# Seven products of halves instead of eight for w_sp times z2, in a one-core FNet and gMLP kernel

## The chip, the cores and the metric

The kernel runs on one core of one Trainium2 chip. The metric is the device time of one execution in microseconds (us), where less is better. Five engines work side by side, each through its own instructions in order, and wait for each other by semaphores: TensorE (PE in the profile; PEld is its weight load), VectorE (DVE), ScalarE (ACT), GpSimd (POOL) and SyncE (SP), which here only issues transfers. Transfers run on 16 DMA engines. TensorE reads its operands from SBUF and sums in PSUM, which has eight banks; one bank holds a 128 x 512 float32 tile.

## What is computed

The input x is 2048 x 512 (S = 2048 rows, D = 512). Everything is float32. Cut to what matters, with `mod` standing for the six rows sa, ca, ga, sb, cb, gb made of `silu(c) @ w_mod`:

```python
h = layernorm(x) * (1 + ca) + sa
y = Cr @ (h @ Hr.T) - Ci @ (h @ Hi.T)       # DFT over 512 columns, then over 2048 rows
x = x + ga * y
h = layernorm(x) * (1 + cb) + sb
z = gelu(h @ w_in)                          # 2048 x 1792
z1, z2 = z[:, :896], layernorm(z[:, 896:])
g = w_sp @ z2 + b_sp[:, None]               # w_sp: 2048 x 2048
x = x + gb * ((z1 * g) @ w_out)             # w_out: 896 x 512
```

## The kernel before

Each float32 product is made of three matmuls on halves of the mantissa (`matmul3`): an operand is split into a high part (a ScalarE copy to float32r) and a low part (a VectorE subtraction), and high x high, high x low and low x high are summed in one PSUM bank. The low x low term is left out.

The program is one list of **steps**, numbered n. A step consumes one moving tile of 128 x 512, which is a 128-wide strip of a large matrix, transposed. `prep(n)` makes the tiles of later steps: `prep_hi(n + 3)` transposes the strip from its block on VectorE (tile `t`) and copies its high part on ScalarE (`ah`), and `prep_lo(n + 2)` subtracts for the low part on VectorE (`al`). There are 2 buffers of `t`, 4 of `ah` and 3 of `al`. A block (`stage`, 512 x 512, two buffers) holds four strips; when its last strip is transposed, `load` has SP fetch the block after the next, by four transfers of 256 KB with rows of 512 bytes. All other work hangs on step numbers: `at(n, f)` puts f behind step n's matmuls in the program, and each engine then follows the program's order.

The stages: 128 steps for the row DFT (`mm_a`, 12 matmuls each, into `gp`), with the column DFT (`mm_y`, into `yp`) between them; 16 steps for z1 (`mm_z1`), whose gelu goes to DRAM (`z1_d`, `z_d` in the profile); 16 for z2 (`mm_z2`), whose rows are normalised and split into `zh` and `zl`; and 64 steps for w_sp times z2. There `mm_w` runs over t, four quarters of 512 rows of w_sp. In a quarter, 16 steps of 7 x 3 = 21 matmuls sum all 2048 rows of z2 into seven banks (`gw`): the weights are 128 x 128 pieces of `zh` and `zl`, the moving tiles are `ah` and `al` of w_sp, and a bank holds 128 columns of z2 by 512 rows of w_sp. At a quarter's end `make_u` adds b_sp on VectorE and multiplies by z1 (on VectorE and GpSimd in turn). While the next quarter runs, `split_u` and `mm_o` multiply with w_out (84 matmuls for a quarter, into `op`), and `add_o` adds x and stores. The last quarter's output (`mm_last`) comes behind the last step.

Of the kernel before, what the change touches and what calls it, by code (L numbers as in the profile page):

```python
# [13 lines left out]
P = 128  # L14
# [5 lines left out]
def fnet_gmlp_kernel(  # L20
# [23 lines left out]

    nc = tc.nc
# [31 lines left out]

# [5 lines left out]
    def matmul3(acc, ah, al, bh, bl, first, last):  # L83
        nc.tensor.matmul(acc, ah, bh, start=first, stop=False)  # L84
        nc.tensor.matmul(acc, ah, bl, start=False, stop=False)  # L85
        nc.tensor.matmul(acc, al, bh, start=False, stop=last)  # L86
# [45 lines left out]
    src += [quad(w_sp, t, g) for t in range(NQ) for g in range(NQ)]  # L132
    NE = 4 * len(src)
# [24 lines left out]
    def prep_hi(n):  # L158
# [4 lines left out]
        if N3 <= n < N4:  # L163
# [26 lines left out]
    hpre = hp.enter_context(pool("hpre"))  # L190
# [315 lines left out]
    def mm_z2(ns):  # L506
# [12 lines left out]
        if k == ND - 1:  # L519
            z = [zrow[0].tile([P, FH], F32, tag="zrow", bufs=4, name=f"z2_{g}_{r}") for r in range(4)]  # L520
# [3 lines left out]
            for r in range(4):  # L524
# [19 lines left out]
    GW, U, UT, X2, BS, OP = {}, {}, {}, {}, {}, {}
    wo_hi, wo_lo = {}, {}

    def load_wo():
        raw = opool[0].tile([P, NF, Q], F32, tag="u", bufs=1, name="wor")
        nc.sync.dma_start(raw, w_out.rearrange("(f p) d -> p f d", p=P))
        for f in range(NF):  # L550
            wraw[f] = raw[:, f, :]
# [17 lines left out]
    def mm_w(ns):

        t, s0 = divmod(ns[0] - N4, NS)
        if s0 == 0:
            for f in range(NF):
                GW[f] = bank(f if t == 0 else (f + 7) % 8, f"gw{t}_{f}")
        a = [(s0 + k, AH.pop(n), AL.pop(n)) for k, n in enumerate(ns)]
        for f in range(NF):
            cols = slice(f * P, (f + 1) * P)
            for s, ah, al in a:
                matmul3(GW[f], z_hi[s][:, cols], z_lo[s][:, cols], ah, al, s == 0, s == NS - 1)

    def make_u(t, f):
        g = opool[0].tile([P, Q], F32, tag="g", bufs=2, name=f"g{t}_{f}")
        nc.vector.tensor_tensor(g, GW.pop(f), BS[t], op=ALU.add)  # L583
        eng = nc.vector if f % 2 else nc.gpsimd
        eng.tensor_tensor(U[t][:, f, :], U[t][:, f, :], g, op=ALU.mult)  # L585

    def make_us(t):
        for f in range(NF):
            make_u(t, f)
            if f == 3:  # L590
                prep(N4 + NS * (t + 1))

    def split_u(t, i):
        uh, ul = UT[t, i] = [opool[0].tile([P, NF, P], F32R, tag=m, bufs=1, name=f"{m}{t}_{i}") for m in ("uh", "ul")]
        nc.scalar.activation(uh, U[t][:, :, i * P:(i + 1) * P], AF.Copy)

    def split_u_lo(t, i):
        uh, ul = UT[t, i]
        nc.vector.tensor_tensor(ul, U[t][:, :, i * P:(i + 1) * P], uh.bitcast(F32), op=ALU.subtract)
# [161 lines left out]
    at(N2 + 5, p2.close)  # L761
# [113 lines left out]
```

## Time and profile before

| | before |
|---|---|
| device time, median of 3 runs | 992.02 us (991.85 to 992.44) |
| the profiled execution | 992.21 us; its span, first to last instruction, 990.4 us |
| TensorE busy | 984.5 us, 99% of the span, 4342 matmuls |
| VectorE, ScalarE, GpSimd busy | 55%, 32%, 14% |
| TensorE in the chain that ended last | 98% |
| transfers | 115.08 MB, 116 GB/s over the span |

Busy time counts when at least one instruction of an engine is in progress. Matmuls are pipelined, so one of 389 ns begins some 0.23 us after the one before it; what a matmul costs is read from the distance of starts, not from its duration. The same holds, to a smaller degree, for VectorE. In the rows of a tile's view stand the shortest, median and longest duration in ns, and the first and the last start in us.

### The profile page before, as it was taken

The numbers are of one execution on the slowest core, as the hardware profiler recorded it, in microseconds if no ns is written. First come the engines' busy times: TensorE is split into PE (matmuls) and PEld (weight loads), VectorE is DVE, ScalarE is ACT, GpSimd is POOL, SyncE is SP. The second block draws the span as 40 slices with busy tenths as digits, with TensorE's granted clock in tenths as the row PEclk, the third lists the DMA queues.
The fourth block names the chain that finished last, engine by engine and source line by source line (L and its number), as shares of the span: only waits on it lengthen the run. The fifth ranks groups of instructions, "written<-read, shape, count | busy, mean of one in ns | idle before, by whom it ended". The sixth has DMA issues, their size and how long they took to land.

```text
span 990.4 us, 11715 instructions
## 1 busy us (share of the span) xinstructions
PE 984.5 (99%) x4342; PEld 815.8 (82%) x4342; DVE 544.8 (55%) x836; ACT 312.0 (32%) x502; POOL 143.5 (14%) x282
## 2 busy tenths in 40 slices
PE   9999999999999999999999999999999999999998
PEld 6888888888888888888888998888888888888886
DVE  7799947775575446557332676566322622262315
ACT  4684424232133123223533775321111111111101
POOL 2330000214310131024311131002000200020001
PEclk9999999999999999999999999999999999999999
DMA  9996544466454535546733332444225223531131
GB/s 209 224 215 136 127 122 89 143 165 174 111 128 86 117 95 128 111 127 151 260 128 117 69 60 43 118 97 127 64 64 159 54 64 75 149 70 47 44 138 43
DMA packets 151642, 115.08 MB, mean 116 GB/s; under 512 B 11424, under 2 KB 132256, under 8 KB 151584
## 3 DMA queue, kind: packets, MB, share of 16 engines
q1 hardware_dynamic: 145088, 93.61, 41.1%
q0 software_dynamic: 6304, 20.46, 5.9%
q8 instruction: 34, 0.56, 0.2%
q10 hardware_dynamic: 192, 0.26, 0.1%
q14 instruction: 24, 0.20, 0.1%
HBM read 94.37 MB, written 19.93 MB: 115 GB/s over the span
## 4 chain that ended last, share of the span: by engine, by line
PE 98%; DMA 1%; DVE 1%; ACT 0%; POOL 0%; issue 0%; SPq 0%; DVEq 0%
PE gp L84 11%; PE gp L85 11%; PE gp L86 11%; PE gw L86 10%; PE gw L85 10%; PE gw L84 10%; PE yp L85 3%; PE yp L84 3%; PE yp L86 3%; PE z2p L84 3%; PE z2p L85 3%; PE z2p L86 3%; PE z1p L84 3%; PE z1p L86 3%; PE z1p L85 3%; PE op L86 2%
## 5 line engine op out<-in xcount | busy, mean ns | idle before, releaser
L170 ACT ACTIVATE ah<-t 128x512 fp32r<-128x512 f32 x224 | 141.5, 632 | 532.0 <-PE gw L86 211.9
L179 DVE TENSOR_TENSOR al<-t,ah 128x512 fp32r<-128x512 f32 x224 | 153.0, 683 | 270.7 <-PE gw L85 138.7
L84 PE MATMUL gp<-ah,hh 128*128 128x512 f32 x496 | 193.3, 390 | 0.0
L85 PE MATMUL gp<-al,hh 128*128 128x512 f32 x496 | 193.3, 390 | 0.0
L86 PE MATMUL gp<-ah,hl 128*128 128x512 f32 x496 | 193.2, 389 | 0.0
L86 PE MATMUL gw<-ah,zl 128*128 128x512 f32 x448 | 174.3, 389 | 0.0
L85 PE MATMUL gw<-al,zh 128*128 128x512 f32 x448 | 174.3, 389 | 0.0
L84 PE MATMUL gw<-ah,zh 128*128 128x512 f32 x448 | 174.3, 389 | 0.0
L147 DVE STREAM_TRANSPOSE t<-stage 128x512 f32<-128x512 f32 x208 | 146.4, 704 | 9.8 <-DMA stage<-in_A_dft_seq_re_dram 4.2
L84 PEld LDWEIGHTS gp<-ah,hh 128*128 128x128 f32 x496 | 93.1, 188 | 19.9
L86 PEld LDWEIGHTS gp<-ah,hl 128*128 128x128 f32 x496 | 93.1, 188 | 19.7
L85 PEld LDWEIGHTS gp<-al,hh 128*128 128x128 f32 x496 | 93.1, 188 | 19.5
L85 PEld LDWEIGHTS gw<-al,zh 128*128 128x128 f32 x448 | 84.1, 188 | 17.6
L84 PEld LDWEIGHTS gw<-ah,zh 128*128 128x128 f32 x448 | 84.1, 188 | 17.4
L86 PEld LDWEIGHTS gw<-ah,zl 128*128 128x128 f32 x448 | 84.1, 188 | 17.4
L585 POOL TENSOR_TENSOR u<-u,g 128x512 f32<-128x512 f32 x16 | 21.4, 1338 | 336.1 <-DVE g L583 336.1
L85 PE MATMUL yp<-htl,gh 128*128 128x512 f32 x128 | 51.1, 399 | 0.0
L84 PE MATMUL yp<-hth,gh 128*128 128x512 f32 x128 | 50.4, 394 | 0.0
L86 PE MATMUL yp<-hth,gl 128*128 128x512 f32 x128 | 50.1, 392 | 0.0
L85 PE MATMUL z2p<-wil,ah 128*128 128x448 f32 x128 | 46.8, 365 | 0.0
L84 PE MATMUL z2p<-wih,ah 128*128 128x448 f32 x128 | 46.7, 365 | 0.0
L86 PE MATMUL z2p<-wih,al 128*128 128x448 f32 x128 | 46.7, 365 | 0.0
(138 smaller groups left out, 1152.1 us busy)
## 6 DMA issues: line engine op xcount, KB each, us to landing
stage<-in_A_dft_seq_im_dram SPq DMA_DIRECT2D x64, 256.0 KB, 5.0
stage<-in_B_w_sp_dram SPq DMA_DIRECT2D x64, 256.0 KB, 4.7
stage<-in_A_dft_seq_re_dram SPq DMA_DIRECT2D x60, 256.0 KB, 4.8
stage<-h_d SPq DMA_DIRECT2D x32, 256.0 KB, 4.9
z_d<-z POOLq DMA_DIRECT2D x28, 256.0 KB, 5.8
u<-z_d SPq DMA_DIRECT2D x4, 1792.0 KB, 8.0
wm<-in_w_mod_dram SPq DMA_DIRECT2D x16, 256.0 KB, 5.8
xr<-in_A_x_dram POOLq DMA_DIRECT2D x16, 256.0 KB, 3.2
```

The lines of the kernel that those rows point to most:

```text
L84: nc.tensor.matmul(acc, ah, bh, start=first, stop=False)
L85: nc.tensor.matmul(acc, ah, bl, start=False, stop=False)
L86: nc.tensor.matmul(acc, al, bh, start=False, stop=last)
L147: nc.vector.transpose(dst.rearrange("p (b i) -> p b i", i=32), block[:, :, 32 * k:32 * k + 32])
L170: nc.scalar.activation(AH[n], T[n], AF.Copy)
L179: nc.vector.tensor_tensor(AL[n], T.pop(n), AH[n].bitcast(F32), op=ALU.subtract)
L585: eng.tensor_tensor(U[t][:, f, :], U[t][:, f, :], g, op=ALU.mult)
```

## The change

The four quarters become two halves, and w_sp and z2 are each cut in two both ways. Write A11, A12, A21, A22 for the 1024 x 1024 quarters of w_sp, and B11, B12, B21, B22 for those of z2, where the columns are cut into 512 and 384 (F1 and F2). Eight products of quarters would give the result; the change takes the seven of Winograd's form, with these sums (a missing 128 columns count as zero):

- of w_sp: S1 = A21 + A22, S3 = A11 - A21, S2 = S1 - A11, S4 = A12 - S2. `load_s` fetches 128 rows of both halves at a time (a unit; 16 of 1 MB), `sum_s` makes the four sums by four VectorE operations, and GpSimd's queue stores them to DRAM (`s_d`). Units 0 to 7 stand at steps 90, 94, ... 118 (in the DFT stage, in place of the pool `hpre`), units 8 to 15 at steps N2 + 6, N2 + 9, ... (the z1 and z2 stages).
- of z2: `sum_t23` and `sum_t14`, in place, by 32 VectorE operations in products 1, 7 and 4.

The products run in the order 1, 6, 7, 4, 5, 3, 2. Each takes 16 steps: eight 128-row pieces of its z2 operand times two 512-wide halves r of its w_sp operand. Products 1, 6, 4, 2 have four blocks of 128 columns (12 matmuls a step), products 7, 5, 3 three (9 a step). Banks 0 to 3 serve r = 0 and 4 to 7 serve r = 1. Products 6, 7, 4 and 3 go on summing in the banks of the product before; what stands there is first copied out by ScalarE (`keep_w`, after products 1, 6, 7, 4) or added to an earlier result by VectorE (`add_w`, after 5, 3, 2). A block of w_sp or of a sum is now 512 rows by two strips of 64 columns, loaded by eight transfers of 128 KB with rows of 256 bytes (`load_half`). The split of z2's operands into high and low is done anew for each product (`hi_b`, `lo_b`). b_sp is added on GpSimd (`add_bs`, 28 operations), w_out is scaled there (`scale_wo`), and all 16 output blocks (`mm_o`, 336 matmuls) follow the last step.

```diff
-    src += [quad(w_sp, t, g) for t in range(NQ) for g in range(NQ)]
-    NE = 4 * len(src)
+    PROD = (1, 6, 7, 4, 5, 3, 2)
+    NE = N4 + 4 * NQ * len(PROD)
+    NB = {p: N4 + 4 * NQ * i for i, p in enumerate(PROD)}
...
+            for r in range(2):
+                load_half(stage[b][:, r], s_d[S_OF[p], r, g] if p in S_OF else
+                          quad(w_sp, r + (2 if p == 4 else 0), g + (0 if p == 1 else 2)), h)
...
+    def sum_s(r, g, b, first):
+        a11, a12, a21, a22 = [SJ[r, g, b][:, i] for i in range(4)]
+        if first:
+            nc.vector.tensor_tensor(a22, a21, a22, op=ALU.add)
+            nc.vector.tensor_tensor(a21, a11, a21, op=ALU.subtract)
+            done = (1, a22), (3, a21)
+        else:
+            nc.vector.tensor_tensor(a11, a22, a11, op=ALU.subtract)
+            nc.vector.tensor_tensor(a12, a12, a11, op=ALU.subtract)
+            done = (2, a11), (4, a12)
+        for m, a in done:
+            nc.gpsimd.dma_start(s_d[m, r, g][b * P:(b + 1) * P, :], a)
...
+    def mm_w(n):
+        i, m = divmod(n - N4, 4 * NQ)
+        p, k, r = PROD[i], m // 2, m % 2
+        nf = 4 if p in (1, 6, 4, 2) else 3
+        fresh = p in (1, 5, 2)
+        if k == 0 and fresh:
+            for f in range(nf):
+                GW[r, f] = bank(4 * r + f, f"gw{p}_{r}_{f}")
+        ah, al = AH.pop(n), AL.pop(n)
+        for f in range(nf):
+            cols = slice(f * P, (f + 1) * P)
+            matmul3(GW[r, f], BH[p, k][:, cols], BL[p, k][:, cols], ah, al, fresh and k == 0, k == 7, not fresh)
+        if k == 7:
+            {1: keep_w, 6: keep_w, 7: keep_w, 4: keep_w}.get(p, add_w)(p, r)
...
+    def load_wo(f):
+        wor[f] = opool[0].tile([P, D], F32, tag="wor", bufs=2, name=f"wor{f}")
+        nc.sync.dma_start(wor[f], w_out[f * P:(f + 1) * P, :])
...
+    for i, u in enumerate((r, g, b) for g in range(2) for b in range(4) for r in range(2)):
+        n = 90 + 4 * i if i < 8 else N2 + 6 + 3 * (i - 8)
+        at(n, load_s, *u)
+        at(n + 3, sum_s, *u, True)
+        at(n + 4, sum_s, *u, False)
...
+        n = NB[3] + 2 + 2 * f
+        at(n, load_wo, f)
+        at(n + 4, scale_wo, f)
+        at(n + 6, make_wo, f)
+        at(n + 7, make_wo_lo, f)
```

How the program's order moves, at three places. First, SP's queue in the last quarter of the row DFT. Before, it holds nothing but block loads:

```order
L139 DMA stage_3002<-in_A_dft_seq_re_dram 32x16x128 x4
L139 DMA stage_3127<-in_A_dft_seq_re_dram 32x16x128 x4
L139 DMA stage_3277<-in_A_dft_seq_im_dram 32x16x128 x4
L139 DMA stage_3410<-in_A_dft_seq_im_dram 32x16x128 x4
L139 DMA stage_3508<-in_A_dft_seq_im_dram 32x16x128 x4
L139 DMA stage_3589<-in_A_dft_seq_im_dram 32x16x128 x4
```

After the change a unit of w_sp (`sj`, two transfers of 512 KB) stands ahead of each block:

```order
L572 DMA sj_3280<-in_B_w_sp_dram 128x2x512 x2
L151 DMA stage_3333<-in_A_dft_seq_im_dram 32x16x128 x4
L572 DMA sj_3439<-in_B_w_sp_dram 128x2x512 x2
L151 DMA stage_3477<-in_A_dft_seq_im_dram 32x16x128 x4
L572 DMA sj_3545<-in_B_w_sp_dram 128x2x512 x2
L151 DMA stage_3586<-in_A_dft_seq_im_dram 32x16x128 x4
```

So each DFT block is now issued behind 1 MB of w_sp, which itself waits until the stores of two units earlier have landed.

Second, VectorE during w_sp times z2. Before, in the second quarter, two or three steps' transposes (`t`) and low parts (`al`) stand between the output's operations, and each step has 21 matmuls or more:

```order
L147 STREAM_TRANSPOSE t_6330<-stage_6151 128x512
L179 TENSOR_TENSOR al_6334<-t_6295,ah_6297 128x512
L147 STREAM_TRANSPOSE t_6379<-stage_6151 128x512
L179 TENSOR_TENSOR al_6383<-t_6330,ah_6332 128x512
L607 TENSOR_TENSOR x2r_2_6328<-op_2_6357,x2r_2_6328 128x512
L147 STREAM_TRANSPOSE t_6411<-stage_6151 128x512
L179 TENSOR_TENSOR al_6415<-t_6379,ah_6381 128x512
L599 TENSOR_TENSOR ul_3_6409<-u_5920,uh_3_6408 128x896
```

After, in product 3 with its 9 matmuls a step, the low parts of z2 (`bl`) and of w_out (`wol`) stand between:

```order
L207 TENSOR_TENSOR al_7635<-t_7597,ah_7599 128x512
L677 TENSOR_TENSOR wol_7626<-wor_7494,woh_7625 128x512
L173 STREAM_TRANSPOSE t_7647<-stage_7515 128x512
L207 TENSOR_TENSOR al_7651<-t_7631,ah_7633 128x512
L613 TENSOR_TENSOR bl_6_7662<-z_3_2_5568,bh_6_7623 128x384
L173 STREAM_TRANSPOSE t_7672<-stage_7515 128x512
L207 TENSOR_TENSOR al_7676<-t_7647,ah_7649 128x512
L677 TENSOR_TENSOR wol_7667<-wor_7539,woh_7666 128x512
L173 STREAM_TRANSPOSE t_7688<-stage_7515 128x512
```

There is an operation more on every step, and a step is under half as long in matmuls.

Third, SP's queue around w_out. Before, w_out comes whole, in the first quarter:

```order
L549 DMA wor<-in_B_w_out_dram 128x7x512
L139 DMA stage_5727<-in_B_w_sp_dram 32x16x128 x4
L139 DMA stage_5860<-in_B_w_sp_dram 32x16x128 x4
L565 DMA u_5920<-z_d_84 128x7x512
L567 DMA bs_5922<-in_B_b_sp_dram 128x512
L139 DMA stage_5994<-in_B_w_sp_dram 32x16x128 x4
```

After, it comes in seven pieces (`wor`, two buffers) in products 3 and 2, between the blocks and the z1 rows (`z1t`):

```order
L666 DMA wor_7494<-in_B_w_out_dram 128x512
L157 DMA stage_7515<-s_d_01_101 32x16x64 x4
L157 DMA stage_7515<-s_d_11_103 32x16x64 x4
L666 DMA wor_7539<-in_B_w_out_dram 128x512
L658 DMA z1t_0_7575<-z_d_86 128x4x512
L666 DMA wor_7578<-in_B_w_out_dram 128x512
L658 DMA z1t_0_7595<-z_d_86 128x3x512
L157 DMA stage_7601<-in_B_w_sp_dram 32x16x64 x8
L666 DMA wor_7629<-in_B_w_out_dram 128x512
L666 DMA wor_7670<-in_B_w_out_dram 128x512
L157 DMA stage_7692<-in_B_w_sp_dram 32x16x64 x8
```

The third piece (`wor_7578`) must wait until VectorE has made `wol_7626` of the first, and the block `stage_7601` is behind it.

More of the change, by code (lines that the diff above doesn't have):

```diff
@@ L544, in fnet_gmlp_kernel, with load_s @@
[L544 to L551, printed above, removed]
+    SJ = {}
+    def load_s(r, g, b):
+        SJ[r, g, b] = spre[-1].tile([P, 4, Q], F32, tag="sj", bufs=4 if len(spre) > 1 else 2, name=f"sj{r}{g}{b}")
+        for i in range(2):
+            v = w_sp.rearrange("(i r) (j c) -> i r j c", i=2, j=2)[i]
+            o = r * Q + b * P
+            nc.sync.dma_start(SJ[r, g, b][:, 2 * i:2 * i + 2], v[o:o + P][:, :, g * Q:(g + 1) * Q])
@@ new lines, in keep_w, with add_w @@
+    def keep_w(p, r):
+        if p in (1, 4):
+            G[p, r] = spre[-1].tile([P, 4, Q], F32, tag="sj", bufs=4, name=f"g{p}_{r}")
+        else:
+            G[p, r] = gpool[0].tile([P, 3, Q], F32, name=f"g{p}_{r}")
+        for f in range(G[p, r].shape[1]):
+            nc.scalar.activation(G[p, r][:, f, :], GW[r, f], AF.Copy)
+    def add_w(p, r):
+        g = G[{5: 7, 3: 6, 2: 1}[p], r]
+        for f in range(g.shape[1]):
+            nc.vector.tensor_tensor(g[:, f, :], GW[r, f], g[:, f, :], op=ALU.add)
@@ new lines, in load_bs, with add_bs, load_z1 @@
+    def load_bs():
+        BS = gpool[0].tile([P, NQ, Q], F32, name="bs")
+        nc.sync.dma_start(BS, b_sp.rearrange("(t q) -> t q", q=Q).partition_broadcast(P))
+        for t in range(NQ):
+            wor["bs", t] = BS[:, t, :]
+    def add_bs(p, r, f):
+        g = G[p, r][:, f, :]
+        nc.gpsimd.tensor_tensor(g, g, wor["bs", r if p in (1, 6) else 2 + r], op=ALU.add)
+    def load_z1(p, r):
+        f0, f1 = (0, 4) if p in (1, 4) else (4, NF)
+        Z1T[p, r] = gpool[0].tile([P, 4, Q], F32, tag="z1t", bufs=2, name=f"z1t{p}_{r}")[:, :f1 - f0]
+        nc.sync.dma_start(Z1T[p, r], z1_d[r if p in (1, 6) else 2 + r][f0:f1].rearrange("f p t -> p f t"))
@@ L569, in mm_w @@
[L569 to L585, printed above, removed]
@@ L605, in add_o, with load_x2 @@
+    def load_x2(t):
+        last = blocks.tile([P, 4, D], F32, tag="stage", bufs=2, name=f"x2r{t}")
+        nc.sync.dma_start(last, x2_d[t].rearrange("(i p) d -> p i d", p=P))
+        for i in range(4):
+            X2[t, i] = last[:, i, :]
     def add_o(t, i):
@@ L829, in fnet_gmlp_kernel @@
-    first_part(0)
-    for f in range(NF):
-        if f + 1 < NF:
-            first_part(f + 1)
-        ul[f] = blocks.tile([P, Q], F32R, tag="al", bufs=3, name=f"ul{f}")
-        nc.vector.tensor_tensor(ul[f], U[t][:, f, :], uh[f].bitcast(F32), op=ALU.subtract)
-        for i in range(4):
-            if f == 1 and i == 3:
-                mm_last(0, 3)
-            if f or i < 3:
-                mm_last(f, i)
-        if f == 0:
-            run(NE)
-    for i in range(4):
-        X2[t, i] = last[:, i, :]
-        add_o(t, i)
+    load_x2(2)
@@ new lines, in fnet_gmlp_kernel @@
+    load_x2(3)
+    for o in range(len(order)):
+        if o == 1:
+            load_z1(1, 0)
+            load_z1(6, 0)
+        if o == 4:
+            load_z1(1, 1)
+            load_z1(6, 1)
+        if o + 1 < len(order):
+            split_u(*order[o + 1])
+            split_u_lo(*order[o + 1])
+        mm_o(*order[o], o % 2)
+        run(NE + o)
+        if o:
+            add_o(*order[o - 1])
+        if o in (4, 8):
+            load_x2(o // 4 - 1)
+        if 2 <= o < 4:
+            for f in range(2):
+                make_u(1, 0, 2 * (o - 2) + f)
+        if o == 4:
+            for f in range(3):
+                make_u(6, 0, f)
+        if 5 <= o < 7:
+            for f in range(2):
+                make_u(1, 1, 2 * (o - 5) + f)
+        if o == 7:
+            for f in range(3):
+                make_u(6, 1, f)
```

189 lines of the change are left out of this document (115 added, 74 removed).

## The prediction

> **What bounds the kernel now.** I read the page first: engines, slices, chain.
>
> ```profile
> span 990.4 us, 11715 instructions
> PE 984.5 (99%) x4342; PEld 815.8 (82%) x4342; DVE 544.8 (55%) x836; ACT 312.0 (32%) x502; POOL 143.5 (14%) x282
> ...
> PE   9999999999999999999999999999999999999998
> ...
> DVE  7799947775575446557332676566322622262315
> ...
> PEclk9999999999999999999999999999999999999999
> DMA  9996544466454535546733332444225223531131
> ...
> PE 98%; DMA 1%; DVE 1%; ACT 0%; POOL 0%; issue 0%; SPq 0%; DVEq 0%
> ```
>
> TensorE is busy in every slice at the full granted clock, and the chain that ended last is TensorE for 98%. VectorE is idle for about three quarters of the last third (slices 28 on), DMA for more. So the number of matmuls sets the time, as long as the others keep up. What one matmul costs comes from the views of the tiles `gw` and `op`, by first and last start.
>
> ```profile
> L84 PE MATMUL gw<-ah,zh x448: 389/389/393, 605.8 to 966.9; 128*128 128x512 f32 x150
> ...
> L86 PE MATMUL op<-woh,ul x112: 388/389/390, 701.5 to 986.4; 128*128 128x512 f32 x112
> ```
>
> Each tile has three such lines, so 3 x 448 + 3 x 112 = 1680 matmuls start between 605.8 and 986.4: 380.6 / 1679 = 0.2267 us each, with no gap left for waits. The duration of 389 ns is not the price; by it the whole kernel would take 1.7 ms.
>
> **The matmuls.** Seven products of 16 steps: four with 12 matmuls a step, three with 9, so 64 x 12 + 48 x 9 = 1200 `gw` matmuls for 1344. It is 144 and not the 168 of one eighth, because 7 column blocks are cut into 4 and 3. The 336 of the output stay and only move. 144 x 0.2267 = **32.6 us less**, if TensorE never waits. A step shrinks from 21 x 0.2267 = 4.76 us to 2.72 us (four blocks) or 2.04 us (three), and the rest of this part asks whether the others follow at that pace. w_sp times z2 then takes 64 x 2.72 + 48 x 2.04 = 272 us.
>
> **VectorE.** Its price per operation, from a stretch of the timeline where it runs without a pause (start, duration):
>
> ```profile
> 684.39 1.27 DVE L583 TENSOR_TENSOR g<-gw,bs 128x512 f32<-128x512 f32 x2
> ...
> 691.58 0.71 DVE L147 STREAM_TRANSPOSE t<-stage 128x512 f32<-128x512 f32 x1
> 692.21 0.65 DVE L179 TENSOR_TENSOR al<-t,ah 128x512 fp32r<-128x512 f32 x1
> 692.78 1.08 DVE L599 TENSOR_TENSOR ul<-u,uh 128x896 fp32r<-128x896 f32 x1
> 693.78 0.70 DVE L147 STREAM_TRANSPOSE t<-stage 128x512 f32<-128x512 f32 x1
> ```
>
> By starts: transpose 0.63, low part 0.57, 896 columns 1.00 (so 384 columns about 0.43, an estimate), an addition from PSUM 0.64. A step needs 1.20. GpSimd's additions disturb it:
>
> ```profile
> L585 POOL TENSOR_TENSOR u<-u,g 128x512 f32<-128x512 f32 x16 | 21.4, 1338 | 336.1 <-DVE g L583 336.1
> ...
> L179 DVE TENSOR_TENSOR al<-t,ah 128x512 fp32r<-128x512 f32 x224 | 153.0, 683 | 270.7 <-PE gw L85 138.7 <-PE gp L85 67.1 <-PE z1p L85 31.6
> ...
> L585 DVE TENSOR_TENSOR u<-u,g 128x512 f32<-128x512 f32 x12 | 14.9, 1239 | 0.4
> ```
>
> The VectorE operations of line 585 that run beside GpSimd's take 1239 ns where the like of line 179 takes 683, so a GpSimd addition costs VectorE about 0.56 us. The Trainium skill's page "SBUF — State Buffer", section "Who interferes with whom", says more: a VectorE operation with two SBUF inputs and a reading GpSimd operation exclude each other for a whole instruction. By that, an estimate is 1.3 us for each, which is rival A's upper end below.
>
> Product by product, VectorE against TensorE: a product has 16 x 1.20 = 19.2 us of steps and eight `bl` (4.6, or 3.4 with 384 columns).
> - Product 1: 23.8, 16 sums of z2 6.9, the last norms some 5.6: 36 of 43.5 us.
> - Product 6: 23.8 and 8 GpSimd additions 4.5: 28 of 43.5. Product 7: 22.6, 6 additions 3.4, three sum pairs 3.0: 29 of 32.6. Product 4: 23.8, five pairs 5.0, 3.4: 32 of 43.5.
> - Product 5: 22.6, 8 additions 4.5, 6 `add_w` 3.8: 31 of 32.6. Product 3: 22.6, 3.8, four `wol` 2.3, five `scale_wo` 2.8: 31.5 of 32.6.
> - Product 2: 23.8, 8 `add_w` 5.1, 14 `make_u` 8.0, three `wol` 1.7, the rest 2: 41 of 43.5.
>
> All fit, 5 and 3 barely; tiles made two to three steps ahead (4 to 8 us) even out bunches. I take 0 to 1 us of waits. By full durations (0.70 + 0.68 a step) products 5, 3 and 2 would lack some 2, 3 and 1.5 us: +6.5, the upper bound; below nothing there is no gain, since TensorE has no other wait to lose.
>
> **Banks handed over.** After products 1, 6, 7, 4 ScalarE copies each bank, as it does here, in 0.6 us:
>
> ```profile
> L80 ACT ACTIVATE gh<-gp x32: 578/598/611, 84.6 to 429.6; 128x512 fp32r<-128x512 f32 x32
> ```
>
> Copies of r = 0 lie beside the last step of r = 1 (2.04 us or more), and the next product needs bank 0 first. Cost 0; if ScalarE comes a whole copy late at each of five hand-overs, 3 us.
>
> **Block loads.** Rows of 256 bytes instead of 512, eight transfers a block. The trace has that size: the very first block is fetched in halves. In the window 9.3 to 11.5 us nearly all packets are of it:
>
> ```profile
> DMA packets 2002, 0.52 MB, mean 238 GB/s; under 512 B 1932, under 2 KB 1996, under 8 KB 2002
> ...
> 10.00:11.00 1.00, 1.00 (x6) 0.83 (x5) 1.00 (x3) 0.96 (x3) 0.00 (x0) 1.00 1.19 265
> 727.50:729.50 2.00, 2.00 (x10) 1.66 (x9) 0.00 (x0) 0.00 (x0) 0.00 (x0) 1.00 1.01 243
> ```
>
> The last column is GB/s: 265 with small packets, 243 in a window of a w_sp block with 512-byte rows. Bytes count, not packets, so 1.05 MB takes 4.4 us of every 8.2 us (4 x 2.04) or 10.9 us. In time from issue to landing:
>
> ```profile
> L139 SPq DMA_DIRECT2D stage<-in_B_w_sp_dram x64: 311/486/3985, 565.6 to 890.3; - x64
> ...
> DMA to landing us min/median/max: 2.3/3.7/6.2
> ```
>
> Seven issues of 0.49 us ahead and 3.7 for the last (the second row is for tiles `stage` up to 14 us, most of them the small ones): 7.1 us, where five steps lie between the issue and the first transpose of that block, 10.2 us with three column blocks. Cost 0. The page "DMA: Bandwidth & Descriptors" of the Trainium skill, section "Specifications", speaks against it: under 512 bytes a transfer doesn't reach line rate, because it reads, modifies and writes. The trace's loads into SBUF don't show it; rival C is what it would do.
>
> **SP's queue.** The wait of `wor_7578` for `wol_7626` holds block 64 (`stage_7601`) back from step 8 to about step 9.5 of product 3; its first transpose is wanted by step 13, and can slip to 15 before TensorE sees it. That leaves 3.5 steps, 7.1 us, against those 7.1 us of loading, plus the 768 KB of z1 just ahead (3.2 us at 243 GB/s). It is the tightest place: 0 to 4 us, I take 1.
>
> **Sums of w_sp.** 64 operations of 0.6 us lie beside the DFT (8 units, some 109 us) and z stages; VectorE there, third number:
>
> ```profile
> 388.00:400.00 12.00, 12.00 (x55) 9.94 (x54) 7.28 (x11) 3.49 (x6) 0.00 (x0) 1.00 0.71 152
> 400.00:412.00 12.00, 12.00 (x55) 9.93 (x54) 6.49 (x10) 2.85 (x5) 0.00 (x0) 1.00 0.55 111
> ```
>
> 12 us gain 2.9 us of VectorE (10.2 at most) and 2.3 MB of units and stores. 152 + 192 = 344 GB/s is above the 243 of block loads, though 2 KB rows run faster:
>
> ```profile
> 632.00:636.00 4.00, 4.00 (x20) 3.30 (x19) 0.69 (x1) 0.63 (x1) 0.00 (x0) 1.00 1.05 375
> ```
>
> Four steps need 1.05 / 0.243 + 2.1 / 0.375 = 9.9 of 10.9 us. At 243 for all it would be 13.0, and 2.1 us lost in each of the four units without a column DFT between: 0 to 8 us; I take 0.5, nearest to the rows of 2 KB.
>
> **The end.** 16 output blocks of 21 matmuls take 4.76 us each, against two `ul` (1.0), an `add_o` (0.7) and up to three `make_u` (1.7) on VectorE: hidden. The last addition and store stay:
>
> ```profile
> L607 DVE TENSOR_TENSOR x_last<-op,x_last x4: 691/692/692, 984.8 to 986.8; 128x512 f32<-128x512 f32 x4
> ```
>
> From 986.8 to the span's end is 3.6 us before, and as much after.
>
> **Sum.** 992.2 of the profiled execution (span 990.4 and 1.8 around it) - 32.6 + 0.5 (VectorE) + 1.0 (SP) + 0.5 (DMA) = 961.6. That execution is 0.2 above the median of 992.0, so I say **961.4 us**.
>
> **Rivals.**
> - A, VectorE becomes the bound in products 5, 3, 2 (7 too, with 1.3 us for each GpSimd addition): +6.5 to +14, 966 to 973. For it: margins of 1 to 2 us. Against: the starts above, which already stand in a dense stretch.
> - B, loads come late, behind `wor` in product 3 or behind the units in the DFT: +4 to +12, 963 to 972. For it: both sums above sit at their limit. Against: VectorE hardly waits for a load now (the transposes' whole idle time is 9.8 us):
>
> ```profile
> L147 DVE STREAM_TRANSPOSE t<-stage 128x512 f32<-128x512 f32 x208 | 146.4, 704 | 9.8 <-DMA stage<-in_A_dft_seq_re_dram 4.2 <-DMA stage<-in_A_dft_seq_im_dram 2.2 <-DVE al L179 0.8
> ```
>
> - C, the other side: small rows run far below the window at 10 us, and each of 28 blocks sets the pace. It decides at 304.7 / 28 = 10.9 us a block (now 304.7 us of `gw` matmuls), 96 GB/s. Two windows' worth of that size ran at 238 and 265, so it would need DRAM sums or the doubled count to behave otherwise. At 12 us a block: 28 x 12 - 272 = +64, 1025 us. By the skill's rule at half of 243 GB/s, an estimate, a block takes 8.6 us, and 12 x 0.5 = +6: still faster.
> - D, the change doesn't do what it says: the count of matmuls in the program is 1200, so no.
>
> **Chances.** Forecast (960 to 963.5) 0.57; A 0.16; B 0.17; C with a slower end 0.06, with a milder one (973 to 990) 0.03; within 0.2% of before, about what a measurement can tell, 0.01. Faster 0.93, same 0.01, slower 0.06. The floor, with no wait at all, is 992.0 - 32.6 = 959.4, and the runs before lie 0.6 apart; the range 958.8 to 973 leaves out C and little else.
>
> **What would show it.** Right: 1200 `gw` matmuls; TensorE busy 99%, and starts 0.2267 us apart through all seven products; VectorE dense in 5, 3 and 2 with little idle, ScalarE under half busy. A: in the waits, TensorE or its weight load waits for `al` in products 5 and 3, with VectorE at 100%. B: VectorE's transposes wait for transfers of `stage`, in product 3, product 2's start or between 290 and 400 us. C: the same in every block, and a landing of 10 us or more. The forecast fails if several waits meet, or if a wait that I put at 0 returns with each of 112 steps.

## The result: 964.4 us, 27.8 us faster

| | before | after |
|---|---|---|
| device time, median | 992.19 us (991.85 to 992.44) | 964.43 us (963.91 to 964.98, 4 runs) |
| ratio to before | | 0.972, 95% interval 0.9708 to 0.9732 |
| the profiled execution | 992.21 us | 964.28 us |
| its span | 990.4 us | 962.5 us |

The forecast was 961.4 us with a range of 958.8 to 973: the time lies in the range, 3.0 us above the forecast. It lies above the 960 to 963.5 us that had the chance of 0.57, and within the 963 to 972 of rival B. The page of the changed kernel, the same lines as shown of before:

```profile
span 962.5 us, 12362 instructions
PE 953.6 (99%) x4198; PEld 788.1 (82%) x4198; DVE 690.4 (72%) x1082; ACT 370.4 (38%) x631; POOL 218.4 (23%) x365
...
PE   8999999999999999999999999999999999999998
...
DVE  7789947785566757856555576888689699897642
...
PEclk9999999999999999999999999999999999999999
DMA  9996652666446797994778964445454456774441
...
PE 93%; DMA 2%; DVE 2%; SPq 1%; issue 1%; ACT 0%; DVEq 0%
```

There are 144 matmuls less (4198 for 4342). VectorE went from 55% to 72%: it is 60 to 90% busy and more in slices 29 to 38, where it had been 20 to 30% busy in eight of ten. TensorE's share of the chain fell from 98% to 93%, and transfers, VectorE and SP's queue took its place there. So something waits, though the tenths of the slices don't show it. Where it waits is shown by the four products behind the first three, one window each (4, 5, 3, 2; the columns are length, then busy time with the number of instructions of PE, PEld, DVE, ACT, POOL, then granted clock, DMA share, GB/s):

```profile
725.10:769.20 44.10, 43.85 (x194) 35.99 (x193) 36.66 (x53) 18.65 (x34) 11.32 (x8) 1.00 0.42 96
769.20:802.20 33.00, 32.95 (x145) 26.96 (x144) 29.28 (x41) 13.92 (x26) 8.61 (x6) 1.00 0.57 128
802.20:835.30 33.10, 33.04 (x146) 27.04 (x144) 28.79 (x46) 15.05 (x27) 5.46 (x4) 1.00 0.73 191
835.30:882.20 46.90, 44.60 (x191) 35.58 (x192) 44.26 (x70) 16.22 (x29) 4.49 (x4) 1.00 0.70 202
```

192 matmuls at 380.6 / 1679 = 0.22668 us are 43.52 us and 144 are 32.64. By the first starts of each product, to a hundredth, the time above these is: products 1, 6 and 7 together 0.07 us, product 4 0.54, product 5 0.34, product 3 0.44, product 2 3.40. That is 4.8 us in all, where the forecast had put 2.0, and nearly three quarters of it is in product 2.

There are two places. The first is the boundary of products 3 and 2. Here are SP's queue and then VectorE (start, duration, idle before in brackets):

```profile
816.09 0.38 SPq L658 DMA_DIRECT2D z1t<-z_d  x1
822.30 0.34 SPq L666 DMA_DIRECT2D wor<-in_B_w_out_dram  x1
822.70 0.42 SPq L658 DMA_DIRECT2D z1t<-z_d  x1
823.17 7.97 SPq L157 DMA_DIRECT2D stage<-in_B_w_sp_dram  x8
```

```profile
821.59 0.68 DVE L677 TENSOR_TENSOR wol<-wor,woh 128x512 fp32r<-128x512 f32 x1
...
831.55 0.71 DVE L173 STREAM_TRANSPOSE t<-stage 128x512 f32<-128x512 f32 x1 [2.57 <-DMA stage<-in_B_w_sp_dram]
...
834.70 1.87 DVE L643 TENSOR_TENSOR g<-gw,g 128x512 f32<-128x512 f32 x3
836.50 1.36 DVE L613 TENSOR_TENSOR bl<-z,bh 128x512 fp32r<-128x512 f32 x1
```

SP issues nothing from 816.5 until VectorE has made the `wol` of 821.59. Then come a piece of w_out, the z1 rows, and block 64 with its eight transfers. The block's first transpose starts at 831.55, and VectorE has waited 2.57 us for it. It doesn't win them back: from there it is busy for 32.39 of 32.45 us, and TensorE pays for what is late.

```profile
831.55:864.00 32.45, 30.09 (x128) 23.23 (x127) 32.39 (x50) 12.44 (x22) 5.49 (x4) 1.00 0.71 180
```

TensorE's own rows there, and its waits over the seven products (in total, times, longest):

```profile
835.52 0.47 PE L95 MATMUL gw<-ah,bh 128*128 128x512 f32 x1 [0.28 <-ACT bh L608]
835.83 0.39 PE L96 MATMUL gw<-al,bh 128*128 128x512 f32 x1
837.91 0.50 PE L97 MATMUL gw<-ah,bl 128*128 128x512 f32 x1 [1.69 <-DVE bl L613]
```

```profile
PE gw L97 <- DVE bl L613: 1.9, 2, 1.7
PE gw L96 <- DVE al L207: 0.3, 1, 0.3
PE gw L95 <- ACT bh L608: 0.3, 1, 0.3
```

From 835.83 to 837.91 is 2.08 us where 0.23 is usual: the low part of product 2's first piece of z2 stands behind product 3's three additions, and then takes 1.36 us instead of 0.68, while GpSimd scales two pieces of w_out (834.30 to 837.31). The sums of waits (2.5 us) are less than the 4.8, since the end of a matmul is modelled and one behind a gap has a longer duration; the starts are what counts.

The second place is at the starts of products 4 and 5, where GpSimd adds b_sp. Of product 4 first GpSimd, then VectorE beside it:

```profile
723.13 9.66 POOL L653 TENSOR_TENSOR g<-g,bs 128x512 f32<-128x512 f32 x6 [24.98 <-ACT g L637]
```

```profile
723.55 1.43 DVE L207 TENSOR_TENSOR al<-t,ah 128x512 fp32r<-128x512 f32 x1
724.90 1.65 DVE L598 TENSOR_TENSOR z<-z,z 128x384 f32<-128x384 f32 x1
726.58 1.66 DVE L599 TENSOR_TENSOR z<-z,z 128x512 f32<-128x512 f32 x1
728.16 0.70 DVE L173 STREAM_TRANSPOSE t<-stage 128x512 f32<-128x512 f32 x1
728.79 1.15 DVE L207 TENSOR_TENSOR al<-t,ah 128x512 fp32r<-128x512 f32 x1
729.87 1.77 DVE L613 TENSOR_TENSOR bl<-z,bh 128x512 fp32r<-128x512 f32 x1
```

The six additions hang on steps in the program's order, but GpSimd has nothing else that paces it: it waits 25 us for the first copy of a bank and then runs all six as one burst. Beside it VectorE's operations with two SBUF inputs take 1.2 to 1.8 us instead of 0.55 to 0.68, while its transposes keep their 0.70. TensorE then waits for that `bl`, 0.4 us more than its usual distance, at 731.7.

### The profile page after: what moved, and what is told of

The parts are those of the page before. It is cut to its first block, busy times and chain, and to the rows that moved or that the text cites. A ratio compares the mean times of both kernels' runs of the same rounds, so it can differ in the third digit from the quotient of the medians.

```text
span 962.5 us, 12362 instructions
## 1 busy us (share of the span) xinstructions
PE 953.6 (99%) x4198; PEld 788.1 (82%) x4198; DVE 690.4 (72%) x1082; ACT 370.4 (38%) x631; POOL 218.4 (23%) x365
## 4 chain that ended last, share of the span: by engine, by line
PE 93%; DMA 2%; DVE 2%; SPq 1%; issue 1%; ACT 0%; DVEq 0%
PE gp L95 12%; PE gp L96 12%; PE gp L97 12%; PE gw L97 8%; PE gw L96 8%; PE gw L95 8%; PE yp L96 3%; PE yp L95 3%; PE yp L97 3%; PE z2p L96 3%; PE z2p L95 3%; PE z2p L97 3%; PE z1p L95 3%; PE op L97 3%; PE z1p L96 3%; PE op L95 3%
## 5 line engine op out<-in xcount | busy, mean ns | idle before, releaser
L207 DVE TENSOR_TENSOR al<-t,ah 128x512 fp32r<-128x512 f32 x272 | 191.4, 704 | 134.0 <-PE gp L96 47.5
L173 DVE STREAM_TRANSPOSE t<-stage 128x512 f32<-128x512 f32 x256 | 180.1, 704 | 13.1 <-DMA stage<-in_A_dft_seq_re_dram 5.1
L97 PE MATMUL gw<-ah,bl 128*128 128x512 f32 x400 | 156.2, 391 | 2.1 <-DVE bl L613 1.9
L96 PE MATMUL gw<-al,bh 128*128 128x512 f32 x400 | 155.9, 390 | 0.3 <-DVE al L207 0.3
L95 PE MATMUL gw<-ah,bh 128*128 128x512 f32 x400 | 155.9, 390 | 0.3 <-ACT bh L608 0.3
L97 PEld LDWEIGHTS gw<-ah,bl 128*128 128x128 f32 x400 | 75.1, 188 | 19.5 <-DVE bl L613 4.0
L96 PEld LDWEIGHTS gw<-al,bh 128*128 128x128 f32 x400 | 75.1, 188 | 16.4 <-DVE al L207 1.0
L95 PEld LDWEIGHTS gw<-ah,bh 128*128 128x128 f32 x400 | 75.1, 188 | 16.3 <-ACT bh L608 0.7
L653 POOL TENSOR_TENSOR g<-g,bs 128x512 f32<-128x512 f32 x28 | 44.0, 1607 | 118.0 <-ACT g L637 118.0
L585 POOL DMA_DIRECT2D s_d<-sj x64 | 35.3, 551 | 125.6 <-DVE sj L577 91.8
```

Of the source, the lines that this page charges most:

```text
L95: nc.tensor.matmul(acc, ah, bh, start=first, stop=False, skip_group_check=go_on)
L96: nc.tensor.matmul(acc, ah, bl, start=False, stop=False, skip_group_check=go_on)
L97: nc.tensor.matmul(acc, al, bh, start=False, stop=last, skip_group_check=go_on)
L173: nc.vector.transpose(dst.rearrange("p (b i) -> p b i", i=32), block[:, :, 32 * k:32 * k + 32])
L207: nc.vector.tensor_tensor(AL[n], T.pop(n), AH[n].bitcast(F32), op=ALU.subtract)
L585: nc.gpsimd.dma_start(s_d[m, r, g][b * P:(b + 1) * P, :], a)
```

## The experiments

Two theories stood after this. **Q**: SP's queue, held by the third piece of w_out, makes block 64 late, and the rest follows. **V**: VectorE has too much to do around the boundary (additions of product 3, products with z1, low parts of w_out), and has it with the block in time as well. GpSimd's burst was a third cause, for products 4 and 5. Of the rivals on record, C (short rows) and the price of the sums of w_sp had to be settled too. "Excess" below is a product's time above its count of matmuls times 0.2267, from the profiled run.

**Three buffers for the pieces of w_out**, so that the third load waits for nothing:

```diff
-        wor[f] = opool[0].tile([P, D], F32, tag="wor", bufs=2, name=f"wor{f}")
+        wor[f] = opool[0].tile([P, D], F32, tag="wor", bufs=3, name=f"wor{f}")
```

> The changed kernel with three buffers for the pieces of w_out in place of two, so that SyncE hardly waits for VectorE's low part of an earlier piece before it can issue block 64 of w_sp. Theory Q (the queue): of the 4.7 us that TensorE lost in the seven products, product 2's 3.4 us come from block 64, which SyncE issued 4.6 us late. Then product 2 takes 43.5 to 44.3 us instead of 46.9, the transposes no longer wait 2.6 us for a transfer of w_sp, and the time is 961.0 to 961.8 us. Rival V (VectorE): at the start of product 2 VectorE has too much to do (additions from PSUM, low parts of z2 and of w_out, products with z1, held up by GpSimd's scaling of w_out), and the late block is beside the point. Then product 2 stays above 46 us and the time at 964.0 +- 0.4 us.

Measured: 963.03 us (962.15 to 963.98), ratio 0.9706 (0.9693 to 0.9719). SP's queue, TensorE's only wait from 800 us on, and VectorE behind the boundary:

```profile
818.53 8.62 SPq L157 DMA_DIRECT2D stage<-in_B_w_sp_dram  x8
```

```profile
PE gw L96 <- DVE al L207: 0.5, 1, 0.5
```

```profile
836.00:848.00 12.00, 11.34 (x47) 8.31 (x47) 12.00 (x19) 3.80 (x7) 2.59 (x2) 1.00 0.60 142
```

Block 64 is issued 4.6 us earlier, no transpose waits for w_sp, and product 3's excess is gone (0.44 to 0). But product 2 keeps 1.70 of 3.40, with VectorE busy for all of these 12 us. So Q, with block 64 in time, accounts for about half of the loss there. That the other half is VectorE's is argued from its being busy without a break; the next runs bear on it. Neither theory's forecast came out (961.0 to 961.8 us and 964.0).

**Without GpSimd's additions of b_sp and its scaling of w_out:**

```diff
-            at(NB[6] + 2 + 4 * r + f, add_bs, 1, r, f)
-            at(NB[5] + 2 + 8 * r + 2 * f, add_bs, 4, r, f)
-            if f < 3:
-                at(NB[7] + 2 + 3 * r + f, add_bs, 6, r, f)
-                at(NB[4] + 2 + 3 * r + f, add_bs, 7, r, f)
+            pass
...
-        at(n + 4, scale_wo, f)
```

> The changed kernel without GpSimd's 28 additions of b_sp and its seven products of w_out with gb: both are left out of the result. The SyncE queue is as in the changed kernel. Theory Q: the 0.5 and 0.3 us lost at the start of products 4 and 5 go, since they stand beside bursts of GpSimd additions; product 2 still loses 2.0 to 3.4 us behind block 64; time 962.0 to 963.5 us. Rival V: without GpSimd VectorE's operations with two SBUF inputs run in 0.57 to 0.68 us throughout, product 2 falls to 44 us or less, and the time to 960.0 to 961.0 us.

Measured: 961.78 us (961.46 to 962.93), ratio 0.9697 (0.9684 to 0.971). The excess of products 4, 5 and 3 is 0, that of product 2 is 2.10. SP still issues nothing until 821.34, and the transposes still wait 2.6 us for w_sp. So the 0.9 us of products 4 and 5 went with GpSimd's additions. Product 5's 0.34 isn't there each time, though: in two runs below, without the sums of w_sp and with one long wait, product 5 loses nothing while the same burst of eight additions runs. Product 2 lost 0.9 to 1.3 us less than in the changed kernel's two profiles (3.40 and, below, 3.00); `scale_wo` is the GpSimd work that lies there.

**Both at once.** Three buffers, and VectorE adds b_sp while it copies the banks, in place of ScalarE's copy and GpSimd's addition:

```diff
     def keep_w(p, r):
...
-            nc.scalar.activation(G[p, r][:, f, :], GW[r, f], AF.Copy)
+            nc.vector.tensor_tensor(G[p, r][:, f, :], GW[r, f], wor["bs", r if p in (1, 6) else 2 + r], op=ALU.add)
...
-        wor[f] = opool[0].tile([P, D], F32, tag="wor", bufs=2, name=f"wor{f}")
+        wor[f] = opool[0].tile([P, D], F32, tag="wor", bufs=3, name=f"wor{f}")
...
```

> The changed kernel with three buffers for w_out's pieces, and with b_sp added by VectorE while it takes the banks out of PSUM (in place of ScalarE's copy), so that GpSimd's 28 additions go; the result is complete. Theory Q with bursts of GpSimd as the cause of the small losses: products 4 and 5 lose under 0.1 us, product 2 under 0.8, time 960.0 to 960.8 us, 0.4% below the changed kernel. Rival V: the 28 additions more on VectorE (18 us in all) make products 5 and 2 worse by 1 to 3 us, time 963 to 966 us.

Measured: 961.93 us (960.78 to 962.63), ratio 0.9694 (0.9681 to 0.9707). That is 1.1 us more than theory Q had forecast at most, and less than rival V's 963 to 966. Its profiled run was its fastest; the excess there is 0.80 us, all in product 2, against 1.70 with three buffers alone, though nothing of the b_sp additions lay in product 2. Runs of each of these two kernels lie 1.8 us apart, so what VectorE costs in product 2 is known to about 1 us only. VectorE took 28 operations more and the kernel is faster than the changed one: an addition from PSUM keeps its duration beside GpSimd (in the changed kernel the three at 834.70 take 1.87 us while `scale_wo` runs), and no burst is left in products 4 and 5.

**Short rows in the kernel before.** Its w_sp blocks come by eight transfers of 256-byte rows, and nothing else differs.

```diff
-            load_block(stage[b], src[b])
+            if 4 * b >= N4:
+                load_block(stage[b], src[b], 0, 64)
+                load_block(stage[b], src[b], 64, P)
+            else:
+                load_block(stage[b], src[b])
```

> The kernel before, with each block of w_sp fetched by eight transfers of rows of 256 bytes instead of four of 512, and nothing else changed. If bytes count and not rows: the same time, 991.6 to 992.6 us, a block's transfers at 230 to 265 GB/s, landings of 3 to 4 us for 128 KB. If short rows ran at half rate (the rival that was forecast to make the change slower): the time stays too, since a block has 19 us here, but a landing of 128 KB takes 5 us or more, and in the window of a block the GB/s fall to 120 to 130.

Measured: 992.26 us (991.92 to 992.43) beside 992.16, ratio 1.0 (0.9991 to 1.0009). One window with a block in it, with short rows and then in the kernel before (DMA share and GB/s are the last two numbers), and how long a 128 KB transfer takes to land (median, last):

```profile
723.00:735.00 12.00, 12.00 (x55) 9.94 (x54) 4.05 (x6) 1.80 (x3) 0.00 (x0) 1.00 0.52 131
```

```profile
723.00:735.00 12.00, 12.00 (x54) 9.95 (x53) 4.25 (x6) 2.01 (x3) 0.00 (x0) 1.00 0.58 131
```

```profile
stage<-in_B_w_sp_dram SPq DMA_DIRECT2D x96, 128.0 KB, 3.1
```

Both windows hold the same bytes (131 GB/s over 12 us), and the DMA engines are no busier with short rows (0.52) than without (0.58). Between rows of 256 and of 512 bytes it is the bytes that count and not the packets, so rival C is excluded. In the changed kernel too, blocks from DRAM sums and from w_sp land alike:

```profile
stage<-s_d SPq DMA_DIRECT2D x128, 128.0 KB, 2.9
...
stage<-in_B_w_sp_dram SPq DMA_DIRECT2D x96, 128.0 KB, 3.2
```

**Without the sums of w_sp.** Neither loads, sums nor stores of units; the products read w_sp itself:

```diff
-                load_half(stage[b][:, r], s_d[S_OF[p], r, g] if p in S_OF else
-                          quad(w_sp, r + (2 if p == 4 else 0), g + (0 if p == 1 else 2)), h)
+                load_half(stage[b][:, r],
+                          quad(w_sp, r + (2 if p == 4 else 0), g + (0 if p == 1 else 2)), h)
...
-        at(n, load_s, *u)
-        at(n + 3, sum_s, *u, True)
-        at(n + 4, sum_s, *u, False)
+        pass
```

> The changed kernel without the sums of w_sp: no units are loaded, summed or stored, and products 5, 6, 7 and 3 read quarters of w_sp itself, so the result is not the reference's. If the 64 operations and 33.6 MB are hidden, as TensorE's starts in the DFT and z stages say: the same time, 964.4 +- 0.8 us. If they cost as I allowed (0.5, at most 8 us): 963.9 or as low as 956.

Measured: 963.94 us (963.73 to 964.27), ratio 0.9714 (0.9697 to 0.973), beside 964.43 and (below) 964.91 for the changed kernel. 64 VectorE operations and 34 MB of transfers (32 of 512 KB, 64 of 256 KB) cost 0.5 to 1.0 us at most, and the intervals don't tell that from nothing. The excess here is 0.56 us in product 4, nothing in product 5, and in products 3 and 2 as large as ever (0.68 and 2.94), so the loss there isn't theirs. The z1 stage's first matmul starts at 451.6 us in the changed kernel and at 451.8 before: the DFT lost nothing to the units.

**The matmuls put back.** In products 7, 5 and 3 the third column block is summed twice, 12 matmuls a step as in the others:

```diff
+        if nf == 3:
+            cols = slice(2 * P, 3 * P)
+            matmul3(GW[r, 2], BH[p, k][:, cols], BL[p, k][:, cols], ah, al, False, False, True)
```

> The changed kernel with a fourth block of matmuls again in products 7, 5 and 3 (the third block once more, which falsifies the sums): 1344 gw matmuls, as many as before, with everything else of the change in place. If the gain is the count of matmuls alone: 959.4 + 32.6 = 992.0 us plus what is lost in waits, 992.0 to 995.5; products 5 and 3 lose nothing now, since their steps have 2.72 us, and product 2 loses less than 2 us. If the change gained or lost elsewhere (the outputs gathered at the end, the sums), the time lies outside by that much.

Measured: 992.69 us (992.12 to 993.84) beside 992.3, ratio 1.0005 (0.9995 to 1.0014). The matmuls of each of the three lines stand at 448 again:

```profile
L95 PE MATMUL gw<-ah,bh x448: 388/389/395, 605.7 to 909.9; 128*128 128x512 f32 x150
```

With the count as before the time is as before, with all that the change adds. No product's excess is over 0.10 us, and TensorE's waits are gone: where a step of products 7, 5 and 3 gives the others 2.72 us instead of 2.04, they keep up. So the gain is the count alone, and the waits come from the short steps.

**Without the products with z1 for half of the result.** The 14 `make_u` of product 2 go, 8 us of VectorE by the prediction's price:

```diff
-        at(NB[2] - 2 + f, make_u, 4, 0, f)
-        at(NB[2] + 6 + f, make_u, 4, 1, f)
-        if f < 3:
-            at(NB[2] + 3 + f, make_u, 7, 0, f)
-            at(NB[2] + 11 + f, make_u, 7, 1, f)
+        pass
```

> The changed kernel without the 14 products with z1 (make_u of products 4 and 7) that VectorE does in product 2; half of the result lacks that factor. The loads of z1, the two buffers of w_out and all of SyncE's queue stay. Of product 2's 3.4 us, three buffers for w_out took away 1.7 and dropping GpSimd's operations took away 1.3, so neither theory holds alone. Theory QV (both meet: the late block leaves VectorE no lead, and VectorE's own surplus in the last two steps of product 3 and the first eight of product 2, 27.7 us of work for 25.9, keeps it from catching up): product 2 loses 1.0 to 2.0 us, the waits after 838 us go, time 962.6 to 963.6. If the surplus is not in these products but in the additions from PSUM, product 2 still loses 2.8 us or more, time 964.0 to 964.6.

Measured: 964.09 us (962.48 to 965.93), ratio 0.9715 (0.9699 to 0.9731): no gain that the runs show, and 2.91 us of excess in product 2. In the expectation's terms that is the second outcome, a surplus that isn't in the products with z1. But a cost that no theory had named is in it, as the profiled run (964.98) shows. SP issued block 64 at 823.89 (at 823.17 and, in the second profile below, 823.51 in the changed kernel), TensorE waited 1.3 us for product 3's additions and 1.0 us for `bl`, and then this (the number ahead of the last two is the granted clock):

```profile
837.02 0.40 PE L96 MATMUL gw<-al,bh 128*128 128x512 f32 x1
838.42 0.80 PE L97 MATMUL gw<-ah,bl 128*128 128x512 f32 x1 [1.00 <-DVE bl L613]
839.01 0.63 PE L95 MATMUL gw<-ah,bh 128*128 128x512 f32 x1
839.44 0.63 PE L96 MATMUL gw<-al,bh 128*128 128x512 f32 x1
```

```profile
838.00:839.00 1.00, 0.58 (x1) 0.50 (x2) 1.00 (x3) 0.00 (x0) 0.00 (x0) 0.62 1.24 278
839.00:840.00 1.00, 1.00 (x4) 0.79 (x3) 1.00 (x2) 0.64 (x1) 0.00 (x0) 0.50 0.57 119
840.00:841.00 1.00, 1.00 (x4) 0.81 (x3) 1.00 (x3) 0.00 (x0) 0.00 (x0) 0.50 0.12 22
841.00:842.00 1.00, 1.00 (x4) 0.76 (x4) 1.00 (x3) 0.00 (x0) 0.00 (x0) 0.67 0.01 2
```

For about 3.4 us (0.76 us of the first window, 0.66 of the last) the clock is halved and starts lie 0.43 us apart. Behind that TensorE never waits again. Eight distances of starts (838.42 to 841.85) take 3.43 us there instead of 1.81. By an estimate that is 1.6 of the 2.91 us, and the 1.3 that stay are what the first outcome had named (1.0 to 2.0). Of the four runs the one with a mean clock of 1.000 is also the fastest, 962.48, and the slowest, 965.93, has 0.997; but a run of the changed kernel at 0.997 took 964.59, no longer than the others. So the run doesn't decide on V; the last experiment measures the halved clock by itself.

**VectorE relieved at the boundary.** As the version with both at once, but with the `make_u` of r = 0 five to eleven steps into product 2, those of r = 1 behind the last step beside the output, and the z1 loads behind the blocks:

```diff
-        at(NB[2] - 2 + f, make_u, 4, 0, f)
-        at(NB[2] + 6 + f, make_u, 4, 1, f)
+        at(NB[2] + 5 + f, make_u, 4, 0, f)
+        at(NE + f // 2, make_u, 4, 1, f)
...
```

> The kernel with three buffers for w_out and b_sp added by VectorE out of PSUM, and the 14 products with z1 moved: those of r = 0 to steps 5 to 11 of product 2, those of r = 1 behind the last step; z1's loads follow them, behind block 65 and later. The result is complete. Theory QV: nothing is left of either cause; product 2 loses under 0.2 us, all seven products stand at their matmuls' time, the profiled span is 957.8 to 958.4 us and the time 959.6 to 961.2. Rival: something else at that boundary (a bank handed over late, GpSimd's scaling of w_out) still costs 0.5 us or more in product 2, and the first output blocks wait for z1 behind the last step by 1 us or more.

Measured: 960.65 us (960.51 to 960.85), ratio 0.968 (0.9666 to 0.9695). The time came out as forecast, but not the reason: the excess is 1.02 us, all in product 2, where the expectation had under 0.2, and its rival (0.5 or more stays) holds. The profile shows no less of it than with both at once (0.80).

**And the pieces of w_out further apart,** every third step instead of every second, with the first low part of products 3 and 2 a step earlier:

```diff
-            at(n - 2, lo_b, p, k)
+            at(n - 2 - (k == 0 and p in (3, 2)), lo_b, p, k)
...
-        n = NB[3] + 2 + 2 * f
+        n = NB[3] + 2 + 3 * f
```

> The kernel of the run before with the moved products (960.65 us), with two more moves around the same place: the seven pieces of w_out come every third step instead of every second, so that two fewer of their low parts and scalings fall into the last steps of product 3 and the first of product 2; and the low part of the first z2 piece of products 3 and 2 stands a step earlier, ahead of the additions from PSUM. If product 2's last 1.0 us is VectorE at its limit between 829 and 842 us: product 2 loses under 0.3 us, span 957.6 to 958.2, time 959.4 to 960.2. Rival: GpSimd's scaling, which still falls beside two operands of VectorE, or the additions that hold bank 0, keep 0.7 us or more; time 960.4 or above.

Measured: **960.15 us** (959.91 to 960.23), ratio 0.9677 (0.9664 to 0.969), the best of all. TensorE's one wait in the seven products, and the 12 us behind the boundary:

```profile
PE gw L97 <- DVE bl L613: 0.3, 1, 0.3
```

```profile
836.00:848.00 12.00, 11.73 (x52) 9.38 (x51) 11.93 (x18) 5.74 (x10) 1.81 (x2) 1.00 0.71 201
```

52 matmuls in these 12 us, against 40 in the changed kernel (9.92 us busy) and 47 with three buffers alone. VectorE is still busy for 11.93 of the 12 us, but TensorE hardly feels it. The excess that is left is 0.56 us, between the under 0.3 that the expectation had and the 0.7 of its rival.

**The changed kernel again**, beside it:

> The changed kernel once more, beside the others on the same chip: 964.4 us +- 0.6, to set the distance of the mended versions against its own spread.

Measured: 964.91 us (964.32 to 965.66), ratio 0.9726 (0.9713 to 0.9739), with an excess of 0.54, 0.34, 0.66 and 3.00 us in products 4, 5, 3 and 2. The loss stands where it stood, and the version above is 4.8 us faster beside it.

**One long wait, made on purpose.** VectorE makes one low part of product 6 fifteen times over, reckoned beforehand as 8.0 us more:

```diff
+        for _ in range(15 if (p, k) == (6, 4) else 1):
             nc.vector.tensor_tensor(BL[p, k][:, :w], b_of(p, k), BH[p, k][:, :w].bitcast(F32), op=ALU.subtract)
```

> The changed kernel with one low part of z2 in product 6 (its fifth) made 15 times instead of once, 14 x 0.57 = 8.0 us more on VectorE at one place, where neither loads nor other engines are late; the result is complete. VectorE is some 2 us ahead of need there, with tiles for two steps more (5.4 us). If a wait costs TensorE only its own length: it waits 1 to 5 us, starts go on at 0.227 us right behind it, and the time grows by that wait. If a wait also lowers the granted clock (as the run without the products with z1 suggests: 0.5 for 3.4 us behind two waits of 1.5 and 1.2 us): the clock falls to 0.5 in the microseconds behind, starts are 0.43 us apart there, and the time grows by 1.5 us or more beyond the wait.

Measured: 972.35 us (970.82 to 974.1), ratio 0.9801 (0.9788 to 0.9815). VectorE's fifteen, TensorE's wait, and the windows behind it:

```profile
666.60 10.86 DVE L614 TENSOR_TENSOR bl<-z,bh 128x512 fp32r<-128x512 f32 x15
```

```profile
671.62 0.39 PE L96 MATMUL gw<-al,bh 128*128 128x512 f32 x1
677.52 0.80 PE L97 MATMUL gw<-ah,bl 128*128 128x512 f32 x1 [5.51 <-DVE bl L614]
678.11 0.63 PE L95 MATMUL gw<-ah,bh 128*128 128x512 f32 x1
```

```profile
674.00:676.00 2.00, 0.00 (x0) 0.00 (x0) 1.93 (x3) 0.00 (x0) 0.00 (x0) 0.81 0.00 0
676.00:678.00 2.00, 0.48 (x1) 0.48 (x2) 1.93 (x4) 0.00 (x0) 0.00 (x0) 0.50 0.00 0
678.00:680.00 2.00, 2.00 (x6) 1.54 (x6) 1.97 (x5) 1.11 (x2) 0.00 (x0) 0.50 0.00 0
680.00:682.00 2.00, 2.00 (x7) 1.54 (x6) 1.36 (x3) 0.67 (x2) 0.00 (x0) 0.50 0.76 173
```

The fifteen took 10.86 us where one takes 0.68, so VectorE had 10.2 us more to do and not 8.0. Of these 5.67 us are TensorE's wait (671.62 to 677.52, less the usual 0.23): the slack there was some 4.5 us, where the expectation had 2. But product 6's excess is 7.98 us, and the other 2.3 us are the halved clock behind the wait.

## Why the prediction was right, and where it was off

- **The matmuls, -32.6 us: right.** 1200 `gw` matmuls (3 x 400), and products 1, 6 and 7 at 0.2267 us each within 0.07 us. With the matmuls put back the time is 992.69. Less the excess of 4.8 us the profiled execution would have taken 959.5, where the prediction had its floor at 959.4.
- **Banks handed over, 0: right where ScalarE copies them.** Products 6, 7 and 4 follow without a gap. Behind product 3 VectorE empties the banks, which the prediction's price didn't look at: TensorE waited for these additions for 0.5 us in the changed kernel's second profile. **Block loads with short rows, 0: right**, by the kernel before with short rows (ratio 1.0). **The end: right**; from the last matmul's end to the span's end it is 3.74 us, for 3.66 before.
- **The sums of w_sp, 0 to 8, taken 0.5: right within what can be told.** The row and column DFT take as long as before, and without the sums the time is 0.5 to 1.0 us less at most.
- **SP's queue, 0 to 4, taken 1.0: the place was right, the size about half.** The prediction named it the tightest place: `wor_7578` waits for `wol_7626` and holds `stage_7601`. The trace shows just this. Block 64 was issued at step 10.2 of product 3, where the prediction had 9.5. Three buffers won 1.4 to 1.9 us by the medians, and 2.1 by the profiles (0.44 + 3.40 - 1.70). "3.5 steps, 7.1 us" against "7.1 us" of loading was no margin, and the eight issues, reckoned at 0.49 each, took 7.97 us together.
- **VectorE, 0 to 1, taken 0.5: this is the step that failed.** "All fit" was reckoned by whole products, and product 2 by "41 of 43.5 us". It was busy 44.26 us of 46.9, and dense for 32.4 us from 831.55 on. The surplus lies not in a product but in the steps on both sides of a boundary, where additions of one product, the first pieces of the next and w_out meet; tiles made 4 to 8 us ahead don't carry over 30 us of dense work. Products 5 and 3, which were to fit barely (31 and 31.5 us), had VectorE busy for only 29.28 and 28.79 us, and product 4, put at 32, for 36.66. With SP's part taken out, 1.7 us stay in product 2 with three buffers and 0.8 with both changes, while VectorE is busy throughout; 0.9 in products 4 and 5 went with GpSimd's additions. So that the place was missed is shown, and the size in product 2 is open by about 1 us. Of the profile before, VectorE was idle for about two thirds of slices 28 to 40 (the busy tenths add up to 42 of 130), not three quarters.
- **A GpSimd addition costs VectorE 0.56 us: too little.** In the burst VectorE needs from 723.55 to 733.34, 9.8 us, for two transposes, one operation of 384 columns and five of 512, which by the prediction's prices take 4.5 (2 x 0.63 + 0.43 + 5 x 0.57). That is 5.3 / 6 = 0.88 us for each addition. The trace gives a value between the prediction's 0.56 and the 1.3 that it had worked out from the Trainium skill, page "SBUF — State Buffer", section "Who interferes with whom"; what that page says of an exclusive pair of ports fits the transposes and additions from PSUM, which keep their duration. That the additions come as a burst wasn't seen at all.
- **The rivals.** B had the place (transposes wait for `stage` at product 2's start), A the other half, but TensorE waits for `bl` (1.9 us) and hardly for `al` (0.3), and in products 4, 5 and 2. Each was priced as a case of its own, 963 to 973; in fact a part of each came together, and made 964.4, a time that the forecast itself had given to B. C and D are excluded; the half rate of C's mildest case was the prediction's own assumption, and short rows had no lower rate here (DMA share 0.52 for 0.58 at the same bytes).

Whether anything of the 0.56 us in the best version can still be won isn't settled, nor how the loss in product 2 divides between VectorE's additions, its products with z1 and GpSimd's `scale_wo`.

## What to carry to other kernels

Where matmuls set the time and fewer of them do the same work, the gain is the count times the distance of starts, and what is at risk is the pace of the engines that feed them: look for the stretch of a few steps around each boundary, not at the sum over a stage. A load that waits for a buffer holds all that stands behind it in SP's queue, so give the small tile one more buffer, or put the large block ahead of it. Work hung on steps runs as a burst where nothing else paces its engine; one VectorE operation from PSUM in place of a copy and an addition on two other engines left products 4 and 5 without a loss here.

## What the runs showed of the hardware that was not expected

A long wait cost TensorE more than its own length. In and behind one of 5.7 us the granted clock was 0.5, until 682 us, with matmuls 0.427 us apart instead of 0.2267, some 2.3 us more. Behind two short waits (1.5 and 1.2 us by the starts, with 0.3 us between) it was halved for about 3.4 us too, while in the changed kernel a wait of 1.9 us, 0.3 us behind one of 0.4, left the clock at 1.00. The Trainium skill, page "TensorE: Matmul & The Clock Gate", Part 1, has the gate fall to half rate after an idle window of about 3.4 us, with 426.7 ns between starts of 512 columns. The distance agrees (0.427), and so does the long wait: a mean of 0.81 from 674 to 676 puts the fall at about 675.2, 3.6 us after the last start. The two short waits are each under that window, so an idle window alone doesn't explain them.
